# Batch 0's first loads cut to three tokens of queries, g loaded as rows, units of the first block reordered, four product tiles moved behind the next block's start

## The chip, the cores and the metric

The kernel runs on one core of a Trainium2 chip. Its engines are TensorE (PE in the profile; PEld is its weight load), VectorE (DVE), ScalarE (ACT), GpSimd (POOL) and SyncE (SP); the loads and stores run on DMA queues that SP, ACT and POOL fill. The metric is the device time of one execution in microseconds (us); lower is better.

## What is computed

Attention with a squared ReLU in place of the softmax, then a feed-forward layer on the normalised tokens, with a residual:

```python
# q, k, v: (8, 12, 448, 64) float32
scores = scale * np.matmul(q, k.transpose(0, 1, 3, 2))        # scale = 1 / sqrt(64)
attn = np.maximum(scores, 0.0) ** 2 / S                        # S = 448
x = np.matmul(attn, v)                                         # -> x (8, 448, 768)
...
mu = np.mean(x, axis=-1, keepdims=True)
var = np.mean((x - mu) ** 2, axis=-1, keepdims=True)
xn = (x - mu) / np.sqrt(var + 1e-06) * g_ln
ch = np.maximum(xn @ w_ch1, 0.0) @ w_ch2                       # 768 -> 3072 -> 768
return x + ch
```

## The kernel before

**Groups and tokens.** The eight batches have twelve heads each. The heads are taken in groups of four: group n is batch n // 3, part m = n % 3, and each batch has G = 3 groups. On the chip a group's q, k or v is a tile of 128 partitions by 2 x 448 columns: two pairs of heads (r = 0, 1), and in each J = 7 "tokens" of D = 64 columns. So a slice of tokens, such as tokens 0 to 2, is 192 columns of each of the two halves; in the source it is a run of 768 bytes per row of a pair, where the whole is 1,792.

**Loads.** Group 0 of batch 0 is fetched in float32 into a staging tile, q by SP's queue and k by ACT's (L149-150), and cast to bf16 afterwards by DVE, ACT and POOL (`cast`, L156-158; POOL casts tokens 3 to 6 of q, L166). All other loads cast on their way and are issued by POOL in the order of L160-171: q and k of groups 1 and 2, v of groups 0 to 2, twelve parts of the weight w1 (six column chunks of 512, two halves each), then group 3 and the next ones. POOL waits now and then before it issues a load: the eleventh went out when the third had landed. `qbuf[m]` holds the queries of part m of batch 0; it has 64 zeroed columns at either end. The vector g is loaded by SP in two transfers, each of 4-byte pieces, straight into `g_sb` (L173-177), and scaled on DVE by `scale_g`.

**Transposes.** Scores need q and k transposed. For batches 0 and 1 PE does that (`transposes`, `piece`): two transposes for each token into PSUM, and a copy by DVE or ACT back to SBUF. For group 0, `idle` matmuls on ones fill PE before the data comes (30, then 2, then 3).

**Blocks.** Batch 0 and batch 1 are cut along the query tokens into two blocks each: batch 0 into query tokens 0 to 2 (`FIRST`) and 3 to 6. A block is a list of units (`attention_block`): for each of its three groups a unit with the scores of key tokens 0 to 3 and a unit with those of 4 to 6, between them (first block of a batch only) the transposes of the next group, then the product with v of the previous group (`values`), and at the end `last` (the last product) and `centre`, which sums over the features by matmuls with ones (L387) and corrects `xc`, the input of the feed-forward layer, in six DVE operations (L393). `scores` leaves the ReLU to ACT (L320) and the squares to DVE: they are put on a list (`later`) and issued by `squares_now`, at the start of a unit, or after one or two product tiles. In `FIRST` nothing else is there for PE, and `busy` puts matmuls between the scores (L285); their input is `qbuf[0][:, D:D + S]`, that is, one half of group 0's queries with all seven tokens. In `FIRST`, tokens 3 to 6 of group 0's queries are transposed just before the last product (L444); those of groups 1 and 2 with all the others of their group.

**Products.** `ffn1_head` makes product tiles 0 to 2 of the first weight together, `ffn1` one tile after the other (six matmuls, L525), so a block has 22 units for 24 tiles. Tiles 20 to 23 need the last chunk of w1. `ffn1` gives the ReLU to DVE (L531) or ACT (L533): `since` counts the tiles since the last scores, and the first one or two go to DVE.

**Order of the work.** All engines run their instructions in the order in which the program puts them. `interleave(main, side, free, ahead)` puts `ahead` side units in front, spreads the others over the main units, and leaves the last `free` main units without any. The program is: the units of `FIRST` one after the other (L626-629); the 22 product units of `FIRST` with the block of query tokens 3 to 6 at their side (L630); w2's loads, into the space that batch 0's working tiles held; the product units of that second block with batch 1's first block at their side (L637), and so on. The second weight's product (`ffn2`, L563) starts at 101.6 us.

PSUM tiles come from two pools: `ps_mm` with two buffers (product tiles, `busy`, transposes of batch 0, the sum of `FIRST`) and `ps_sc` with three (scores, products with v, transposes of batch 1, `idle_ps`).

```python
def busy(n):
    ps = ps_mm.tile([P, 512], fp32, tag="mm", name="busy_ps")
    for _ in range(n):
        nc.tensor.matmul(ps[:, :S], ones, qbuf[0][:, D:D + S], start=True, stop=True)
```

Of the kernel before, what the change touches and what calls it, by code (L numbers as in the profile page):

```python
# [12 lines left out]
def interleave(main, side, free=0, ahead=0):  # L13


    for unit in side[:ahead]:
        unit()
    side = side[ahead:]
    n, done = len(main) - free, 0
    for i, unit in enumerate(main):  # L20
        unit()
        want = min(len(side), (len(side) * (i + 1)) // n)
        while done < want:
            side[done]()
            done += 1
# [3 lines left out]
def kernel(  # L29
# [22 lines left out]
    nc = tc.nc  # L52
    P = 128
    HP = 64
    bf16 = mybir.dt.bfloat16
    fp32 = mybir.dt.float32

    B, H, S, D = q.shape
# [3 lines left out]
    J = S // HP  # L62
    NP = H // 2
    G = NP // 2
    NB = 2 * J + 1
    K1 = d_model // P
# [9 lines left out]
    const = ctx.enter_context(tc.tile_pool(name="const", bufs=1))  # L76
# [16 lines left out]
    nc.vector.memset(ones, 1.0)  # L93


    srcs = {
        n: [t[b].rearrange("(r hh) (p j) d -> (hh p) r (j d)", hh=2, p=HP) for b in range(B)]
        for n, t in (("q", q), ("k", k), ("v", v))
    }
    qkv = {}  # L100
# [7 lines left out]
    def load(n, names):  # L108
        if n >= len(groups):
            return  # L110
        b, m = groups[n]
        for name in names:
            if b == 1 and name != "v":
                o = (2 * m + "qk".index(name)) * 2 * S
                t = hold[:, o:o + 2 * S].rearrange("p (r s) -> p r s", r=2)
            elif name == "q":
                t = qbuf[m][:, D:D + 2 * S].rearrange("p (r s) -> p r s", r=2)
            else:
                t = io.tile([P, 2, S], bf16, tag=name, name=name + "_sb", bufs=4 if name == "v" else 3)
            nc.gpsimd.dma_start(t, srcs[name][b][:, m:NP:G, :])  # L120
            qkv[name, b, m] = t
# [13 lines left out]
    def load_w1(i):  # L135
        s = slice(i * NCH, (i + 1) * NCH)
        for hf in range(2):
            nc.gpsimd.dma_start(w1[hf * HP:(hf + 1) * HP, :, s], w1_src[hf][:, :, s])
# [4 lines left out]

    stage = hpool.tile([P, K2, S2], bf16, tag="hT", name="stage_sb")
    stage = stage.rearrange("p a n -> p (a n)")[:, :8 * S].bitcast(fp32)
    stage = stage.rearrange("p (i r s) -> p i r s", i=2, r=2)
    for i, (queue, name) in enumerate(((nc.sync, "q"), (nc.scalar, "k"))):  # L149
        queue.dma_start(stage[:, i], srcs[name][0][:, 0:NP:G, :])  # L150

    nc.scalar.activation(spool.tile([P, 1], fp32, tag="root", name="root"), eps_sb, ACTF.Sqrt)
    qkv["q", 0, 0] = qbuf[0][:, D:D + 2 * S].rearrange("p (r s) -> p r s", r=2)
# [2 lines left out]
    def cast(copy, name, lo, hi):  # L156
        s = slice(lo * D, hi * D)
        copy(qkv[name, 0, 0][:, :, s], stage[:, "qk".index(name), :, s])

    load(1, "qk")  # L160
    make_identity(nc, identity)
    load(2, "qk")
    load(0, "v")
    load(1, "v")
    load(2, "v")
    cast(nc.gpsimd.tensor_copy, "q", 3, J)  # L166
    for i in range(6):
        load_w1(i)
    load(3, "qkv")
    load(4, "qk")  # L170
    load(5, "qk")

    g_sb = const.tile([P, K1], fp32)  # L173
    g_src = moe_g_ln.rearrange("(hf c p) -> hf p c", hf=2, p=HP)
    with nc.allow_non_contiguous_dma(reason="one vector of 768"):
        for hf in range(2):
            nc.sync.dma_start(g_sb[hf * HP:(hf + 1) * HP, :], g_src[hf])
    g_mean = const.tile([P, K1], fp32)
    g_score = const.tile([P, K1], fp32)

    def scale_g():
        nc.vector.tensor_scalar_mul(g_mean, g_sb, -1.0 / d_model)
        nc.vector.tensor_scalar_mul(g_score, g_sb, score_scale)

# [3 lines left out]
    def idle(n):  # L188

        for _ in range(n):  # L190
            nc.tensor.matmul(idle_ps[:, 0, :P], ones, ones, start=True, stop=True)
# [1 line left out]
    xT, xc = {}, {}  # L193
    st = {}

    def piece(sb, b, m, n, cuts):
        if b == 0:
            ps = ps_mm.tile([P, 1024], bf16, tag="mm", name="tr_ps")
        else:
            ps = ps_sc.tile([P, 2, 1024], bf16, tag="sc", name="tr_ps")[:, 0]  # L200
        src, i = qkv[n, b, m], "qk".index(n)
        for copy, lo, hi in cuts:
            for j in range(lo, hi):
                for pr in range(2):
                    nc.tensor.transpose(  # L205
                        ps[pr * HP:(pr + 1) * HP, j * P:(j + 1) * P],
                        src[:, pr, j * D:(j + 1) * D], identity)
        for copy, lo, hi in cuts:
            copy(sb[:, i * J + lo:i * J + hi, :],
                 ps[:, lo * P:hi * P].rearrange("p (j c) -> p j c", c=P))  # L210

    def transposes(b, m):


        if b == 0:
            o = 12 * 1024 + m * 2 * J * P
            sb = early[:, o:o + 2 * J * P].rearrange("p (i c) -> p i c", c=P)
        elif m:
            o = (m - 1) * 2 * J * P
            sb = hold[:, o:o + 2 * J * P].rearrange("p (i c) -> p i c", c=P)  # L220
        else:
            sb = tpool.tile([P, NB, P], bf16, tag="qT", name="qT_sb")
        dve, act = nc.vector.tensor_copy, nc.scalar.copy
        if (b, m) == (0, 0):

            cast(dve, "q", 0, 3)
            cast(act, "k", 0, 3)
            cast(act, "k", 3, J)
            idle(30)
            piece(sb, b, m, "q", ((dve, 0, 3),))  # L230
            idle(2)
            piece(sb, b, m, "k", ((dve, 0, 3), (dve, 3, J)))
            idle(3)
        elif b == 0:
            piece(sb, b, m, "q", ((dve, 0, J),))
            piece(sb, b, m, "k", ((dve, 0, 3), (act, 3, J)))
        else:
            piece(sb, b, m, "q", ((dve, 0, J),))
            piece(sb, b, m, "k", ((dve, 0, J),))
        squares_now()  # L240
        st[b, m] = {
            "q": lambda i, r: sb[:, 0:J],
            "k": lambda i: sb[:, J + i],
            "where": lambda pr, j: (j, pr),
            "attn": [], "sb": sb}
# [27 lines left out]


    FULL = (0, J)
    BLK = (((0, 3), (3, J - 3)), ((0, 4), (4, J - 4)))
    FIRST = (0, BLK[0][0])
    n_early = [0]

# [13 lines left out]
    def squares_now(n=None):  # L293


        if n is None or n in [k for k, _ in later]:
            for _, a in later:
                nc.vector.tensor_mul(a, a, a)
            later.clear()
# [116 lines left out]
    def attention_block(b, blk):  # L416


        lo, hi, first = b * G, b * G + G, blk[0] == 0
        units = [lambda: transposed(lo)] if first else []  # L420

        def unit(n, part):
            squares_now()
            for i in range(4 * part, min(4 * part + 4, J), 2):
                if (b, blk) == FIRST and (n == G - 1 or n and i == 2):
                    busy(1)
                scores(n, tuple(range(i, min(i + 2, J))), blk)
            if (b, blk) == FIRST and part and n == hi - 1:
                squares_now()
            if b == 1 and not first and part and n == hi - 1:  # L430
                transposed(hi)
            if part and n > lo:
                values(n - 1, blk)
                if not first:
                    load(n + 3, "v")
        for n in range(lo, hi):
            units.append(lambda n=n: unit(n, 0))
            if first and n + 1 < hi:
                units.append(lambda n=n: transposed(n + 1))
            units.append(lambda n=n: unit(n, 1))  # L440

        def last():
            if (b, blk) == FIRST:
                piece(st[0, 0]["sb"], 0, 0, "q", ((nc.scalar.copy, 3, J),))  # L444
            values(hi - 1, blk)
            if (b, blk) == FIRST:
                busy(2)
            if b == 1 and not first:
                load(hi + 3, "v")
        units.append(last)  # L450
        units.append(lambda: centre(b, blk))
        return units
# [148 lines left out]
    def ffn1_units(b, blk=FULL):  # L601
        if blk == FULL:
            return [lambda ni=ni: ffn1(b, ni, blk) for ni in range(K2)]
        return [lambda: ffn1_head(b, blk)] + [lambda ni=ni: ffn1(b, ni, blk) for ni in range(3, K2)]
# [18 lines left out]


    pairs = B // 2
    for i, unit in enumerate(attention_block(0, BLK[0][0])):  # L626
        if i == 2:
            scale_g()
        unit()
    interleave(ffn1_units(0, BLK[0][0]), attention_block(0, BLK[0][1]), 3, 1)  # L630
    w2 = wpool.tile([P, K2, d_model], bf16, tag="w2", name="w2")
    for i in range(4):
        load_w2(w2, i, 4)
    load(6, "qkv")
    load(7, "qk")
    load(8, "qk")
    interleave(ffn1_units(0, BLK[0][1]), attention_block(1, BLK[1][0]), 3, 1)  # L637
    interleave(ffn1_units(1, BLK[1][0]), attention_block(1, BLK[1][1]), 3, 1)
    tokens(0)
    transposed(by_dma * G + 1)  # L640
# [45 lines left out]
```

## Time and profile before

| what | value |
|---|---|
| median of 3 runs | 552.45 us (551.58 to 556.33) |
| the profiled execution | 551.32 us, its span 549.5 us |
| PE busy | 538.7 us, 98% of the span |
| PEld, DVE, ACT, POOL busy | 318.3, 266.0, 260.2, 109.2 us |
| mean granted clock of PE | 0.997 |
| DMA | 56.62 MB moved, 51.91 MB of it read from HBM |

Busy time by stretch of the same execution, in us (PE, DVE, ACT), with the granted clock and what the DMA engines moved:

| stretch | PE | DVE | ACT | clock | GB/s |
|---|---|---|---|---|---|
| 0 to 5 us | 3.38 | 0.47 | 1.49 | 1.00 | 186 |
| 5 to 10 | 3.70 | 2.13 | 2.54 | 0.81 | 179 |
| 10 to 15 | 4.34 | 4.34 | 4.27 | 0.85 | 204 |
| 15 to 20 | 4.29 | 4.25 | 3.95 | 1.00 | 207 |
| 20 to 25 | 4.59 | 2.71 | 3.64 | 1.00 | 205 |
| 25 to 30 | 4.63 | 4.16 | 4.19 | 1.00 | 206 |
| 30 to 35 | 5.00 | 4.44 | 4.78 | 1.00 | 207 |
| 35 to 40 | 4.76 | 3.34 | 2.58 | 1.00 | 204 |
| 50 to 60 | 10.00 | 6.58 | 8.28 | 1.00 | 211 |

How to read it: block `FIRST` runs from the first scores at 7.86 us to the sum at 20.41; its product units and the second block of batch 0 fill the time to 41.5 us. The DMA figures count what is written: a load that casts reads float32 and writes half as many bytes, so 205 GB/s of such loads are 410 GB/s read. In the timeline each line gives the start and the length of a run of equal instructions, the engine, the line, the operation, its output and inputs and, in brackets, how long the engine was idle before and what ended that.

### The profile page before, as it was taken

The page shows a single profiled execution, that of the slowest core. Times are in us where ns is not written, and L with a number is a line of the kernel's source. Part 1 is how long each engine was busy: PE and PEld are TensorE (multiplying, and loading weights), DVE is VectorE, ACT ScalarE, POOL GpSimd, SP SyncE. Part 2 cuts the span into 40 slices and gives each one's busy share as a digit, 9 for nine tenths or more (in the row PEclk, how much of TensorE's full clock was granted, in tenths as well). Part 3 has the DMA queues.
Part 4 walks back from the last instruction along what each step waited for, and adds up shares of the span by engine and source line. Part 5 has one row for each costly group of instructions (what it writes and reads, how often), then busy time and mean ns, then how long its engine had stood idle before and what let it go on. Part 6 is the DMA issues. An engine that isn't in the chain of part 4 may idle for free.

```text
span 549.5 us, 10988 instructions
## 1 busy us (share of the span) xinstructions
PE 538.7 (98%) x4734; PEld 318.3 (58%) x4734; DVE 266.0 (48%) x511; ACT 260.2 (47%) x424; POOL 109.2 (20%) x135
## 2 busy tenths in 40 slices
PE   7899999999999999999999999999999999999997
PEld 5687779655555555555555555555555555555655
DVE  4776753378886250057777532027687670001111
ACT  5776775455553444455545344445545244440000
POOL 7334102024426100003614400001230400000000
PEclk8999999999999999999999999999999999999999
DMA  9999999979999900028999960006941250001222
GB/s 188 207 204 208 210 194 148 117 116 162 164 176 127 212 2 1 0 59 144 123 142 160 173 124 1 0 1 91 170 102 30 60 100 0 1 0 30 58 57 58
DMA packets 107216, 56.62 MB, mean 103 GB/s; under 512 B 77216, under 2 KB 103712, under 8 KB 107168
## 3 DMA queue, kind: packets, MB, share of 16 engines
q1 hardware_dynamic: 79680, 29.77, 32.3%
q0 software_dynamic: 26976, 25.50, 31.7%
q8 instruction: 37, 0.61, 0.5%
q10 hardware_dynamic: 512, 0.66, 0.3%
q14 instruction: 11, 0.09, 0.1%
HBM read 51.91 MB, written 11.01 MB: 115 GB/s over the span
## 4 chain that ended last, share of the span: by engine, by line
PE 90%; DMA 8%; issue 0%; POOL 0%; DVE 0%; SPq 0%; POOLq 0%
PE o_ps L563 38%; PE h_ps L525 38%; PE sc_ps L309 6%; DMA w<-in_moe_w_ch_dram 5%; PE av_ps L339 5%; DMA qT_sb<-q_sb 2%; PE o_ps L588 1%; DMA q_sb<-in_q_dram 1%; PE h_ps L547 1%; PE sum_ps L387 1%; PE tr_ps L205 0%; POOL k_sb L120 0%; POOL q_sb L120 0%; DVE o_sb L591 0%; POOL identity masks.py:199 0%
## 5 line engine op out<-in xcount | busy, mean ns | idle before, releaser
L525 PE MATMUL h_ps<-xc_sb,w 128*128 128x448 bf16 (+2 forms) x1368 | 219.2, 318 | 0.6 <-DVE hT_sb L531 0.4
L563 PE MATMUL o_ps<-w,hT_sb 128*128 128x384 bf16 x1296 | 219.6, 326 | 0.0
L525 PEld LDWEIGHTS <-w 128*128 128x128 bf16 x1368 | 128.6, 98 | 86.9 <-issue 3.1
L563 PEld LDWEIGHTS <-hT_sb 128*128 128x128 bf16 x1296 | 123.1, 98 | 94.2 <-issue 16.0
L320 ACT ACTIVATE attn_sb<-sc_ps 128x896 bf16<-128x896 f32 (+4 forms) x150 | 126.4, 902 | 84.6 <-PE sc_ps L309 84.6
L533 ACT ACTIVATE hT_sb<-h_ps 128x448 bf16<-128x448 f32 (+2 forms) x212 | 102.5, 483 | 121.5 <-PE h_ps L525 121.1
L322 DVE TENSOR_TENSOR attn_sb<-attn_sb 128x896 bf16<-128x896 bf16 x126 | 81.5, 654 | 39.1 <-ACT attn_sb L320 38.2
L569 DVE SCALAR_TENSOR_TENSOR o_sb<-o_ps,rstd_sb,xtok_sb 128x384 f32<-128x384 f32 x54 | 33.0, 611 | 49.1 <-PE o_ps L563 48.7
L510 DVE RECIPROCAL rstd_sb<-rstd_sb 128x1 f32<-128x1 f32 (+1 forms) x10 | 1.7, 168 | 98.0 <-ACT rstd_sb L509 98.0
L504 DVE BATCH_NORM_STATS2 stats<-xtok_sb 128x6 f32<-128x384 bf16 x56 | 27.5, 533 | 32.7 <-DMA xtok_sb<-xT_sb 32.7
L370 POOL TENSOR_TENSOR part_sb<-part_sb,xT_sb 128x448 f32<-128x448 f32 x24 | 29.5, 1229 | 66.9 <-DVE xT_sb L346 59.3
L367 POOL TENSOR_TENSOR part_sb<-xT_sb 128x448 f32<-128x448 bf16 x6 | 6.6, 1106 | 168.6 <-DVE xT_sb L346 138.7
L393 DVE SCALAR_TENSOR_TENSOR xc_sb<-total_sb,g_mean,xc_sb 128x448 bf16<-128x448 f32 (+2 forms) x54 | 29.0, 605 | 21.2 <-ACT total_sb L391 21.2
L309 PE MATMUL sc_ps<-qT_sb,kT_sb 64*64 64x448 bf16 x504 | 34.7, 357 | 1.5 <-DMA qT_sb<-q_sb 1.5
L339 PE MATMUL av_ps<-attn_sb,v_sb 64*64 64x448 bf16 (+2 forms) x672 | 32.3, 327 | 0.0
L346 DVE TENSOR_SCALAR xT_sb<-av_ps 128x896 bf16<-128x896 f32 (+2 forms) x30 | 26.9, 900 | 9.4 <-PE av_ps L339 9.4
L352 DVE TENSOR_SCALAR xc_sb<-xT_sb,g_sb 128x448 bf16<-128x448 bf16 (+2 forms) x56 | 28.6, 558 | 1.0
L339 PEld LDWEIGHTS <-v_sb 64*64 64x64 bf16 x840 | 22.9, 107 | 10.6 <-issue 1.6
L120 POOL DMA_DIRECT2D k_sb<-in_k_dram x20 | 14.2, 713 | 47.0 <-DMA kT_sb<-k_sb 37.0
L309 PEld LDWEIGHTS <-kT_sb 64*64 64x64 bf16 x504 | 11.5, 105 | 18.5 <-issue 15.0
L120 POOL DMA_DIRECT2D v_sb<-in_v_dram x24 | 17.4, 729 | 21.7 <-PE av_ps L339 17.9
L320 ACT ACTIVATE early<-sc_ps 128x768 bf16<-128x768 f32 (+3 forms) x24 | 18.3, 827 | 2.7 <-PE sc_ps L309 2.5
(63 smaller groups left out, 196.1 us busy)
## 6 DMA issues: line engine op xcount, KB each, us to landing
out_dram<-o_sb SPq DMA_DIRECT2D x54, 192.0 KB, 3.6
v_sb<-in_v_dram POOLq DMA_DIRECT2D x24, 224.0 KB, 4.9
w<-in_moe_w_ch_dram POOLq DMA_DIRECT2D x12, 384.0 KB, 14.5
w<-in_moe_w_ch_dram POOLq DMA_DIRECT2D x4, 1152.0 KB, 20.0
q_sb<-in_q_dram POOLq DMA_DIRECT2D x20, 224.0 KB, 7.7
k_sb<-in_k_dram POOLq DMA_DIRECT2D x20, 224.0 KB, 7.2
hold_sb<-in_q_dram POOLq DMA_DIRECT2D x3, 224.0 KB, 11.9
hold_sb<-in_k_dram POOLq DMA_DIRECT2D x3, 224.0 KB, 11.1
```

Source lines behind the costliest of these rows:

```text
L120: nc.gpsimd.dma_start(t, srcs[name][b][:, m:NP:G, :])
L309: nc.tensor.matmul(ps[cols, r, o * w:(o + 1) * w], g["k"](i)[rows, cols], g["q"](i, r)[rows, blk[0]:sum(blk), cols], start=True, stop=True)
L320: nc.scalar.activation(a, ps[:, :, :len(slots) * w], ACTF.Relu)
L322: nc.vector.tensor_mul(a, a, a)
L339: nc.tensor.matmul(ps[cols, hh, :w], v_sb[rows, pr, j * D:(j + 1) * D], g["attn"][i][rows, r, :], start=(j == 0), stop=(j == J - 1))
L352: nc.vector.tensor_scalar_mul(xc[b][:, c, of(blk)], xT[b // 2][:, c, of(blk, b)], g_sb[:, c:c + 1])
L370: nc.gpsimd.tensor_add(part[b], part[b], x[:, c])
L393: nc.vector.scalar_tensor_tensor(xc[b][:, c, of(blk)], total, g_mean[:, c:c + 1], xc[b][:, c, of(blk)], op0=ALU.mult, op1=ALU.add)
L525: nc.tensor.matmul(ps[:, :w], w1[:, c, ni * P:(ni + 1) * P], xc[b][:, c, of(blk)], start=(c == 0), stop=(c == K1 - 1))
L533: nc.scalar.activation(hT[pair][:, ni, o:o + w], ps[:, :w], ACTF.Relu)
L563: nc.tensor.matmul(ps[:, :DH], hT[pair][:, ki, t * P:(t + 1) * P], w2[:, ki, cols], start=(ki == 0), stop=(ki == K2 - 1))
L569: nc.vector.scalar_tensor_tensor(o_sb[t][:, cols].rearrange("p (c d) -> p c d", d=D), ps[:, :DH].rearrange("p (c d) -> p c d", d=D), rstd[ ...
```

## The change

The staging of group 0 is cut: q's tokens 0 to 2 by SP's queue, k's tokens 0 to 2 by ACT's, k's tokens 3 to 6 by SP's after q's. Of q, tokens 3 to 6 are no longer staged, but loaded with a cast by POOL, after v of group 2; of groups 1 and 2 POOL loads q's tokens 0 to 2 where it loaded the whole q, and tokens 3 to 6 after the first chunk of w1. POOL's own cast goes. g is loaded as six rows in one transfer and turned on PE by two small float32 matmuls with a 6 x 6 identity, copied and scaled on DVE before the first scores. k's tokens 3 to 6 of group 0 are transposed after the first scores, q's tokens 3 to 6 of groups 1 and 2 in the second block, each directly before the scores of its group (in a buffer of `ps_sc`), those of group 0 before `last`. In `FIRST` the second scores unit of group 0 goes ahead of the transposes of group 1, and the product of group 1 goes ahead of the last scores unit. Of `FIRST`'s product units the last four are taken out of the interleaving (which now runs over 18 units, leaves one free, and still puts one side unit ahead) and follow the first five units of the next block, whose remaining 17 are interleaved with batch 1's first block.

```diff
@@ -93,6 +93,9 @@
     nc.vector.memset(ones, 1.0)
+    BLK = (((0, 3), (3, J - 3)), ((0, 4), (4, J - 4)))
     srcs = {
         n: [t[b].rearrange("(r hh) (p j) d -> (hh p) r (j d)", hh=2, p=HP) for b in range(B)]
         for n, t in (("q", q), ("k", k), ("v", v))
@@ -143,11 +146,18 @@
     stage = hpool.tile([P, K2, S2], bf16, tag="hT", name="stage_sb")
     stage = stage.rearrange("p a n -> p (a n)")[:, :8 * S].bitcast(fp32)
     stage = stage.rearrange("p (i r s) -> p i r s", i=2, r=2)
-    for i, (queue, name) in enumerate(((nc.sync, "q"), (nc.scalar, "k"))):
-        queue.dma_start(stage[:, i], srcs[name][0][:, 0:NP:G, :])
+    FEW = BLK[0][0][1]
+    def load_uncast(queue, name, lo, hi):
+        s = slice(lo * D, hi * D)
+        queue.dma_start(stage[:, "qk".index(name), :, s], srcs[name][0][:, 0:NP:G, s])
+    load_uncast(nc.sync, "q", 0, FEW)
+    load_uncast(nc.scalar, "k", 0, FEW)
+    load_uncast(nc.sync, "k", FEW, J)
     nc.scalar.activation(spool.tile([P, 1], fp32, tag="root", name="root"), eps_sb, ACTF.Sqrt)
     qkv["q", 0, 0] = qbuf[0][:, D:D + 2 * S].rearrange("p (r s) -> p r s", r=2)
@@ -157,28 +167,38 @@
         s = slice(lo * D, hi * D)
         copy(qkv[name, 0, 0][:, :, s], stage[:, "qk".index(name), :, s])
-    load(1, "qk")
+    def load_queries(m, lo, hi):
+        s = slice(lo * D, hi * D)
+        t = qkv["q", 0, m] = qbuf[m][:, D:D + 2 * S].rearrange("p (r s) -> p r s", r=2)
+        nc.gpsimd.dma_start(t[:, :, s], srcs["q"][0][:, m:NP:G, s])
+    load_queries(1, 0, FEW)
+    load(1, "k")
     make_identity(nc, identity)
-    load(2, "qk")
+    load_queries(2, 0, FEW)
+    load(2, "k")
     load(0, "v")
     load(1, "v")
     load(2, "v")
-    cast(nc.gpsimd.tensor_copy, "q", 3, J)
-    for i in range(6):
+    load_queries(0, FEW, J)
+    load_w1(0)
+    load_queries(1, FEW, J)
+    load_queries(2, FEW, J)
+    for i in range(1, 6):
         load_w1(i)
     load(3, "qkv")
     load(4, "qk")
     load(5, "qk")
+    g_rows = const.tile([K1, 2, HP], fp32)
+    nc.sync.dma_start(g_rows, moe_g_ln.rearrange("(hf c p) -> c hf p", hf=2, p=HP))
     g_sb = const.tile([P, K1], fp32)
-    g_src = moe_g_ln.rearrange("(hf c p) -> hf p c", hf=2, p=HP)
-    with nc.allow_non_contiguous_dma(reason="one vector of 768"):
-        for hf in range(2):
-            nc.sync.dma_start(g_sb[hf * HP:(hf + 1) * HP, :], g_src[hf])
     g_mean = const.tile([P, K1], fp32)
     g_score = const.tile([P, K1], fp32)
+    identity_g = const.tile([K1, K1], fp32)
     def scale_g():
+        nc.vector.tensor_copy(g_sb, idle_ps[:, 1, :K1])
         nc.vector.tensor_scalar_mul(g_mean, g_sb, -1.0 / d_model)
         nc.vector.tensor_scalar_mul(g_score, g_sb, score_scale)
@@ -193,8 +213,8 @@
     xT, xc = {}, {}
     st = {}
-    def piece(sb, b, m, n, cuts):
-        if b == 0:
+    def piece(sb, b, m, n, cuts, first=True):
+        if b == 0 and first:
             ps = ps_mm.tile([P, 1024], bf16, tag="mm", name="tr_ps")
         else:
             ps = ps_sc.tile([P, 2, 1024], bf16, tag="sc", name="tr_ps")[:, 0]
@@ -226,13 +246,19 @@
             cast(dve, "q", 0, 3)
             cast(act, "k", 0, 3)
             cast(act, "k", 3, J)
-            idle(30)
+            nc.vector.tensor_copy(identity_g, identity[:K1, :K1])
+            idle(24)
             piece(sb, b, m, "q", ((dve, 0, 3),))
-            idle(2)
-            piece(sb, b, m, "k", ((dve, 0, 3), (dve, 3, J)))
             idle(3)
+            piece(sb, b, m, "k", ((dve, 0, 3),))
+            for hf in range(2):
+                nc.tensor.matmul(
+                    idle_ps[hf * HP:(hf + 1) * HP, 1, :K1], g_rows[:, hf], identity_g,
+                    start=True, stop=True)
+            idle(3)
+            scale_g()
         elif b == 0:
-            piece(sb, b, m, "q", ((dve, 0, J),))
+            piece(sb, b, m, "q", ((dve, 0, FEW),))
             piece(sb, b, m, "k", ((dve, 0, 3), (act, 3, J)))
         else:
             piece(sb, b, m, "q", ((dve, 0, J),))
@@ -273,7 +299,6 @@
     FULL = (0, J)
-    BLK = (((0, 3), (3, J - 3)), ((0, 4), (4, J - 4)))
     FIRST = (0, BLK[0][0])
     n_early = [0]
@@ -421,15 +446,21 @@
         def unit(n, part):
             squares_now()
+            if b == 0 and not first and part == 0 and n:
+                piece(st[0, n]["sb"], 0, n, "q", ((nc.vector.tensor_copy, FEW, J),), False)
             for i in range(4 * part, min(4 * part + 4, J), 2):
                 if (b, blk) == FIRST and (n == G - 1 or n and i == 2):
                     busy(1)
                 scores(n, tuple(range(i, min(i + 2, J))), blk)
+                if (b, blk) == FIRST and n == i == 0:
+                    piece(st[0, 0]["sb"], 0, 0, "k", ((nc.vector.tensor_copy, 3, J),))
             if (b, blk) == FIRST and part and n == hi - 1:
                 squares_now()
+                piece(st[0, 0]["sb"], 0, 0, "q", ((nc.scalar.copy, FEW, J),))
             if b == 1 and not first and part and n == hi - 1:
                 transposed(hi)
-            if part and n > lo:
+            if n > lo and part == (0 if (b, blk) == FIRST and n == hi - 1 else 1):
                 values(n - 1, blk)
                 if not first:
                     load(n + 3, "v")
@@ -438,10 +469,10 @@
             if first and n + 1 < hi:
                 units.append(lambda n=n: transposed(n + 1))
             units.append(lambda n=n: unit(n, 1))
+        if b == 0 and first:
+            units[2:4] = units[3], units[2]
         def last():
-            if (b, blk) == FIRST:
-                piece(st[0, 0]["sb"], 0, 0, "q", ((nc.scalar.copy, 3, J),))
             values(hi - 1, blk)
             if (b, blk) == FIRST:
                 busy(2)
@@ -623,18 +654,21 @@
     pairs = B // 2
-    for i, unit in enumerate(attention_block(0, BLK[0][0])):
-        if i == 2:
-            scale_g()
+    for unit in attention_block(0, BLK[0][0]):
         unit()
-    interleave(ffn1_units(0, BLK[0][0]), attention_block(0, BLK[0][1]), 3, 1)
+    units = ffn1_units(0, BLK[0][0])
+    interleave(units[:-4], attention_block(0, BLK[0][1]), 1, 1)
     w2 = wpool.tile([P, K2, d_model], bf16, tag="w2", name="w2")
     for i in range(4):
         load_w2(w2, i, 4)
     load(6, "qkv")
     load(7, "qk")
     load(8, "qk")
-    interleave(ffn1_units(0, BLK[0][1]), attention_block(1, BLK[1][0]), 3, 1)
+    late, units = units[-4:], ffn1_units(0, BLK[0][1])
+    for unit in units[:5] + late:
+        unit()
+    interleave(units[5:], attention_block(1, BLK[1][0]), 3, 1)
     interleave(ffn1_units(1, BLK[1][0]), attention_block(1, BLK[1][1]), 3, 1)
     tokens(0)
     transposed(by_dma * G + 1)
```

## The prediction

> **What bounds the kernel now.** First the page's chain of waits, by engine, then the same chain in order of time.
>
> ```profile
> PE 90%; DMA 8%; issue 0%; POOL 0%; DVE 0%; SPq 0%; POOLq 0%
> ```
> ```profile
> 3.37 6.30 DMA q_sb<-in_q_dram
> ...
> 9.95 12.69 DMA w<-in_moe_w_ch_dram
> ...
> 22.93 15.63 DMA w<-in_moe_w_ch_dram
> ...
> 38.70 0.66 PE h_ps L525 x6
> ```
>
> After 40 us the chain is matrix work on PE, which the change leaves as it is. Up to 38.70 us the chain runs through loads. So this is a question about the first 40 us, and a microsecond won or lost there stays. Next the timeline of those 40 us.
>
> ```profile
> 7.86 0.71 PE L309 MATMUL sc_ps<-early 64*64 64x192 bf16 x16 [0.18 <-DVE early L209]
> ...
> 11.12 0.52 PE L285 MATMUL busy_ps<-q_sb,ones 128*128 128x448 bf16 x1
> ...
> 11.98 0.36 PE L309 MATMUL sc_ps<-early 64*64 64x192 bf16 x8 [0.34 <-ACT early L320]
> ...
> 13.35 0.66 POOL L138 DMA_DIRECT2D w<-in_moe_w_ch_dram  x1 [0.43 <-DMA v_sb<-in_v_dram]
> ...
> 19.15 0.73 ACT L350 ACTIVATE xc_sb<-av_ps,g_score 128x192 bf16<-128x192 f32 x2 [0.98 <-DVE xT_sb L346]
> ...
> 20.41 0.66 PE L387 MATMUL sum_ps<-xT_sb,ones 128*128 128x192 bf16 x6 [0.95 <-ACT early L209]
> ...
> 26.17 0.62 DVE L531 TENSOR_SCALAR hT_sb<-h_ps 128x192 bf16<-128x192 f32 x2
> 26.57 0.66 PE L525 MATMUL h_ps<-xc_sb,w 128*128 128x192 bf16 x6 [0.37 <-DVE hT_sb L531]
> ...
> 26.70 1.02 DVE L298 TENSOR_TENSOR early<-early 128x1024 bf16<-128x1024 bf16 x2
> ```
>
> The reader is to see three things: the filler matmul of L285 reads q_sb and ran at 11.12 without waiting for a load; the sum of L387, with which block one ends, came at 20.41; and DVE still works on squares at 27.7 that were due from 26.17 on, so it runs about a microsecond behind PE. Last, the clock, by windows of 1 us (PE busy, granted clock, DMA share, GB/s).
>
> ```profile
> 7.00:8.00 1.00, 0.82 (x19) 1.00 1.43 171
> 8.00:9.00 1.00, 1.00 (x26) 0.53 1.29 194
> ...
> 11.00:12.00 1.00, 0.66 (x13) 0.76 1.26 202
> 12.00:13.00 1.00, 1.00 (x34) 1.00 1.28 213
> ```
>
> PE had been idle for 1.59 us before 6.07; from 8 to about 11.3 it was granted half the clock.
>
> **Part one, the shorter first loads.** The first casts (5.65 us) waited for two loads of 459 KB read each. Now two of 197 KB come first. From 2.8 us the transfers ran at about 400 GB/s, so 524 KB less is 1.3 us. If a row of 768 B costs what one of 1,792 B does, nothing is won: the rows are as many (512). I take 1.2. Four of seven key tiles leave the path (8 transposes, 0.3 us, and a DVE copy of 0.35): 0.6. The page "DMA: Bandwidth & Descriptors" of the Trainium skill (Specifications) speaks against the cut: transfers under 512 B miss line rate, and the cut rows arrive as 384 B of bf16. By that rule the two cut query loads would each cost a whole one, some 1 us together by this trace's 1.1 us a load; no row here shows it.
>
> The rows of g replace 768 pieces of 4 bytes; DVE's 1.15 us wait for them at 9.28 cost little, since the transposes it copied next ended only then. Now PE waits for g instead, ahead of the first scores. It comes third on SP's queue, behind 459 KB; with both cut loads that is 655 KB, landed by about 5.2 us at that rate, where PE is near 5.3: 0, at most 1 us. First scores at 7.86 - 1.8 = 6.0.
>
> **Part two, the filler now waits for a load.** `busy` reads columns D to D+S of qbuf[0], all seven tokens. Tokens 3 to 6 used to be cast by POOL from the staged copy (6.93, 0.66 us). Now they are the eighth POOL load, after v 2. That the kernel's waits follow regions, not tiles, the trace shows: h_ps used w1 at 21.57 while w1's last part came at 38.56. From first scores to first filler took 3.3 us, so PE stands there at 9.3.
>
> When does the tail land? POOL's eleventh load went out when the third had landed (9.67), so the fourteenth, at 13.35, marks the sixth, v 1: about 13.1. To there 917 + 6 x 459 = 3,670 KB were read; to the tail it is 655 + 2 x 197 + 2 x 459 + 3 x 459 + 262 = 3,606 KB. By pieces: 2,048 rows and 768 of g, now 2,816 rows, the same. So 13.1; 12.3 if g's pieces cost the 0.7 us by which the rate sags below 205 GB/s between 5 and 8 us, 14.3 if short rows cost full ones. PE stands still for 3.8 us; behind the filler are queued scores of group 1, all of group 2 and both products.
>
> From 13.1: filler to scores 0.3, scores and six query transposes to 14.0. DVE then has, without a gap, two copies (0.36 each), two squares (0.51 each), xT 0.55, two xc 0.63, squares 0.51 and 0.31: 17.7. Only then can the product of group 1 run, which the change puts ahead of the last scores: 0.8, xT 0.55, then ACT's two xc (0.73; L350 waited for xT before, too), and behind these in ACT's queue the last two activations, 0.65 and 0.36: 20.8. Square 0.3, product 0.8, xT 0.55: 22.5, against 20.41. **+2.1** (0.5 if only ACT's queue counted, which resumes at 13.6 instead of 13.06; 2.8 with the late tail). The 0.95 us before L387, ACT's copy, is gone and is in this.
>
> The clock: 1.59 us idle brought 3.3 us at half; 3.8 us idle should do it again. The same work took 0.96 against 0.58 (14 transposes). From the filler to the end of the first product is some 2.7 us at full clock, 4.3 at half; part is hidden behind DVE. **+1.0** (0 to 2). The page "TensorE: Matmul & The Clock Gate" (Part 1) says that the gate drops after an idle window of about 3.4 us and opens after a busy one; the drop after 1.59 us was earlier than that rule says. By it alone the cost could be 0.
>
> **Part three, the postponed query tiles.** Two times 8 transposes come into block two: 0.3 us each, **+0.6**. They stand directly ahead of the scores that need them, with only DVE's copy between. DVE has that copy behind its evictions and squares: at the first place PE arrives at 26.57, transposes to 26.9, DVE free at 27.7, copy 0.4, scores at 28.2. That is 1.3 us with nothing else for PE. The second, behind xT 0.69, xc 0.48 and squares 1.02, about 0.9. **+2.2** (0.6 to 3).
>
> **Part four, the last four tiles.** They free PE of w1's last part: the wait at 38.70 goes, **-0.25**; with block one late, no other load binds (the parts landed 0.8 to 1.4 us ahead of use). But between the sum of block two and the head that needs its corrections stood three units and 28 transposes, 2.6 us; now it is one unit, 0.66. The first correction ends 0.85 after the sum and six take 2.47, paced at 0.41 against 0.35 on PE: **+0.5** (0.2 to 1.2). The next block's ten side units fall on 14 main units in place of 19; ACT was 8.3 of 10 us busy there: **+0.2** (0 to 1). The late tiles' own work is only moved. w2 is needed at 101; POOL's load at 65.34 waited for one of its four parts, 5 to 6 us apart, so it is there by about 71 and its delay is covered by 30 us.
>
> Sum: 2.1 + 1.0 + 0.6 + 2.2 - 0.25 + 0.5 + 0.2 = 6.35 us. The profiled execution took 551.3; 551.3 + 6.35 = **557.7**. The median shown is 1.1 above that execution, its lowest 0.3; I leave the number.
>
> **Rivals.** *The hold is cheap* (full clock, and DVE has caught up while PE stood, so each copy costs 0.3 us): 2.1 + 0.6 + 0.6 - 0.25 + 0.5 + 0.2 = 3.75, so 555.1. For it: every engine drains during the hold. Against: DVE is refilled by the first squares.
> *Not slower: PE isn't held at L285.* It would take a tail that has landed by 9.3 us, or no wait for it. Then block one ends about 3.8 us earlier than above (22.5 - 3.8 = 18.7), a gain of 1.7. Block two is then paced by w1's parts, whose arrival hardly moves and which had 0.8 to 1.4 us of slack; the copies fall into those waits, and about 0.9 is left, less 0.5 at the head: 551.3 - 0.4 = 550.9. Against it: 3.6 MB by 9.3 us is over 500 GB/s, which no window shows.
> *The hold is dear*: tail at 14.3, half clock for two stretches, copies at their upper ends: +9.5, so 560.8.
>
> **How the numbers follow.** The forecast 0.50 (its own range 555.5 to 560), cheap 0.22, not held 0.15, dear 0.13. Range 551.8 to 560.3, leaving out about half of the not-held and half of the dear case. About 1% (5.5 us) is what a measurement of this kernel can tell from no change; the bound is 558.0. Slower by more: just over half of the forecast (0.28) and the dear case, 0.41. Faster by more would need 5.5 us in a stretch that holds 1.7: 0.02. Within: 0.57.
>
> **What would show it.** Right: a PE idle of some 4 us before the first L285, ended by a q_sb load; half clock after it; L387 near 23; in block two PE waiting at L309 for DVE's L209. Wrong: a first L285 without a wait, L387 before 20, or no new waits of PE between 25 and 45 us.

## The result, and the profile after

| | before | after |
|---|---|---|
| median of 6 runs | 553.09 us (550.99 to 556.33) | 560.76 us (560.31 to 563.26) |
| the profiled execution, its span | 551.32, 549.5 us | 560.31, 558.5 us |
| sum of block one | 20.41 us | 25.82 us |
| first matmul of the second weight's product | 101.47 us | 112.16 us |

The ratio is 1.0152, with a 95% interval of 1.0123 to 1.0181: slower by over 1%. The page's chain of waits by engine, after:

```profile
PE 94%; DVE 2%; DMA 2%; POOL 1%; issue 0%; ACT 0%; POOLq 0%
```

DMA's share of the chain fell from 8% to 2%, and the kernel is slower all the same. The same chain in order of time (start, us, engine, what) shows what stands in its place:

```profile
6.92 9.14 DMA q_sb<-in_q_dram
16.11 0.55 PE busy_ps L310
...
25.98 0.50 PE sum_ps L412 x6
...
32.14 0.93 DVE early L323 x2
33.46 0.63 PE sc_ps L334 x16
...
47.90 0.49 DVE xc_sb L418
48.44 2.47 PE h_ps L578 x18
```

One load of queries, issued at 6.92 us, carries the chain for 9.14 us, to the filler (now L310). Twice more the chain goes over DVE to PE, at 32 and at 48 us. The timeline, in brackets how long the engine was idle before and what ended that:

```profile
16.11 0.55 PE L310 MATMUL busy_ps<-q_sb,ones 128*128 128x448 bf16 x1 [5.07 <-DMA q_sb<-in_q_dram]
17.37 0.96 PE L225 MATMUL tr_ps<-identity,k_sb 128*64 128x128 bf16 x14
...
25.82 0.66 PE L412 MATMUL sum_ps<-xT_sb,ones 128*128 128x192 bf16 x6
...
33.46 0.63 PE L334 MATMUL sc_ps<-early 64*64 64x256 bf16 x16 [1.56 <-DVE early L229]
...
39.60 0.63 PE L334 MATMUL sc_ps<-early 64*64 64x256 bf16 x16 [1.15 <-DVE early L229]
...
48.44 2.47 PE L578 MATMUL h_ps<-xc_sb,w 128*128 128x256 bf16 x18 [0.48 <-DVE xc_sb L418]
...
74.24 0.64 PE L364 MATMUL av_ps<-attn_sb,v_sb 64*64 64x256 bf16 x12 [0.59 <-DVE attn_sb L323]
```

PE is held 5.07 us by the load; waits 1.56 and 1.15 us for DVE's copies of the postponed query tiles (L229); and 0.48 us for the correction at the head of the next block. None of these waits was there before. Two distances divide the loss: **A**, the sum of block one, came 5.41 us later; **B**, from that sum to the second weight's product, grew from 81.06 to 86.34 us, by 5.28. Within B all of it lies ahead of the sum of batch 1's first block (44.37 us after the sum of block one before, 49.65 now); from there to the second product it is 36.69 us in both.

Of these 10.7 us the time shows 9.0 (by the two profiled executions) or 7.7 (by the medians). What is missing in the profiled executions, 1.7 us, is met near 280 us for the most part, where PE waited 1.5 us for transposed queries before and not at all after.

### The profile page after: what moved, and what is told of

It reads as the page before. It is cut to its first block, busy times and chain, and to the rows that moved or that the text cites. A ratio compares the mean times of both kernels' runs of the same rounds, so it can differ in the third digit from the quotient of the medians.

```text
span 558.5 us, 10989 instructions
## 1 busy us (share of the span) xinstructions
PE 542.1 (97%) x4733; PEld 319.6 (57%) x4733; DVE 266.7 (48%) x515; ACT 261.0 (47%) x424; POOL 111.4 (20%) x137
## 3 DMA queue, kind: packets, MB, share of 16 engines
HBM read 51.91 MB, written 11.01 MB: 113 GB/s over the span
## 4 chain that ended last, share of the span: by engine, by line
PE 94%; DVE 2%; DMA 2%; POOL 1%; issue 0%; ACT 0%; POOLq 0%
PE o_ps L594 39%; PE h_ps L556 38%; PE sc_ps L334 7%; PE av_ps L364 6%; DMA q_sb<-in_q_dram 2%; PE h_ps L578 1%; PE o_ps L619 1%; PE sum_ps L412 1%; DVE early L323 1%; PE tr_ps L225 1%; DVE xT_sb L371 0%; POOL v_sb L123 0%; PE busy_ps L310 0%; DVE xc_sb L377 0%; POOL k_sb L123 0%
## 5 line engine op out<-in xcount | busy, mean ns | idle before, releaser
L594 PEld LDWEIGHTS <-hT_sb 128*128 128x128 bf16 x1296 | 123.1, 98 | 94.3 <-issue 16.1
L334 PEld LDWEIGHTS <-kT_sb 64*64 64x64 bf16 x504 | 11.5, 105 | 16.8 <-issue 13.3
```

The costliest lines, as they stand in the source:

```text
L334: nc.tensor.matmul(ps[cols, r, o * w:(o + 1) * w], g["k"](i)[rows, cols], g["q"](i, r)[rows, blk[0]:sum(blk), cols], start=True, stop=True)
L594: nc.tensor.matmul(ps[:, :DH], hT[pair][:, ki, t * P:(t + 1) * P], w2[:, ki, cols], start=(ki == 0), stop=(ki == K2 - 1))
```

## The experiments

All start from the kernel after, but for two that start from the one before. For each: the filler's first matmul, the sum of block one, the start of the second product, B, PE's wait near 280 us, all from one profiled execution (us); then the median and the ratio to the kernel before, run beside it on the same chip (its medians beside e1 to e12 were 551.4 to 552.1 us, so rows are compared by the ratio).

| kernel | filler | sum | 2nd product | B | wait at 280 | median | ratio, 95% |
|---|---|---|---|---|---|---|---|
| before | 11.12 | 20.41 | 101.47 | 81.06 | 1.5 | 553.09 | |
| after | 16.11 | 25.82 | 112.16 | 86.34 | 0 | 560.76 | 1.0152 (1.0123 to 1.0181) |
| e1 filler reads keys | 11.19 | 21.07 | 107.41 | 86.34 | 2.5 | 558.46 | 1.0106 (1.0060 to 1.0152) |
| e2 whole queries | 15.09 | 25.41 | 111.75 | 86.34 | 0.7 | 561.36 | 1.0165 (1.0130 to 1.0201) |
| e3 tiles a unit earlier | 15.38 | 25.01 | 109.45 | 84.44 | 1.8 | 561.89 | 1.0178 (1.0143 to 1.0213) |
| e4 late tiles back | 15.22 | 24.72 | 107.84 | 83.12 | 1.2 | 557.89 | 1.0108 (1.0069 to 1.0147) |
| e5 hold filled | 15.69 | 23.95 | 110.31 | 86.36 | 0 | 561.75 | 1.0162 (1.0121 to 1.0202) |
| e6 before + tail | 15.44 | 25.68 | 106.28 | 80.60 | 1.9 | 556.18 | 1.0068 (1.0046 to 1.0090) |
| e9 = e1+e3+e4 | 11.01 | 20.73 | 102.77 | 82.04 | 1.6 | 553.49 | 1.0031 (1.0004 to 1.0058) |
| e10 = e9 + order | 11.20 | 19.60 | 102.25 | 82.65 | 2.4 | 552.93 | 0.9999 (0.9972 to 1.0027) |
| e11 first loads only | 11.17 | 18.78 | 101.43 | 82.65 | 2.3 | 551.98 | 1.0006 (0.9988 to 1.0023) |
| e12 before + late tiles | 11.01 | 20.47 | 103.56 | 83.09 | 0.7 | 553.75 | 1.0048 (1.0028 to 1.0069) |

**e1: the filler reads keys, which have landed.** Only what fills PE there is changed.

```diff
-        nc.tensor.matmul(ps[:, :S], ones, qbuf[0][:, D:D + S], start=True, stop=True)
+        nc.tensor.matmul(ps[:, :S], ones, qkv["k", 0, 0][:, 0, :], start=True, stop=True)
```

> The changed kernel, but the filler matmuls of L285 (L310 in the changed kernel) read group 0's keys, which are cast by 5.7 us, in place of its queries. Theory (the hold at the filler is the largest loss): PE's 5.1 us wait at the filler is gone, PE's clock isn't halved after it, and the sum that ends block one (25.82 us in the changed kernel, 20.41 before) comes at about 20; time about 555, that is 5.5 us under the changed kernel and 2 over the one before. Rival (DVE and ACT set the pace of block one anyway, and PE only waits for them elsewhere): the sum comes at about 24 and the time is 558 to 559.

Its timeline:

```profile
11.19 0.56 PE L310 MATMUL busy_ps<-k_sb,ones 128*128 128x448 bf16 x1
...
21.07 0.66 PE L412 MATMUL sum_ps<-xT_sb,ones 128*128 128x192 bf16 x6
...
282.87 0.96 PE L334 MATMUL sc_ps<-qT_sb,kT_sb 64*64 64x448 bf16 x8 [2.48 <-DMA qT_sb<-q_sb]
```

The hold is gone, and A with it, all but 0.66 us (the sum was expected at about 20, by the rival at 24); B is unchanged to the hundredth. The filler starts at 11.19 without a wait, though the tail landed at 13.5 us in this profile. So the load held PE through the filler's operand alone. The time, 558.46, lies in the rival's range all the same, for another reason: of the 4.75 us won at the front the profiled execution kept 0.5. PE waited 2.48 us at 282 us, where after it didn't wait, and then ran at half the clock (window: length, PE busy, granted clock, DMA share, GB/s):

```profile
282.00:283.00 1.00, 0.13 (x4) 0.89 1.32 246
283.00:284.00 1.00, 1.00 (x9) 0.50 1.30 229
...
286.00:287.00 1.00, 1.00 (x7) 0.90 1.28 258
```

That is 3.4 us at half, or 1.7 us lost by an engine that is busy. The same is seen in e3, e10 and e11. From the start of the second product to the end, the wait at 280 taken off, it is 447.9 to 448.2 us in these four, where the clock fell after waits of 1.81 to 2.48 us, and 446.3 to 446.8 us in the other eight profiles, where it stayed at 1.00 (e6 waited 1.90 us and kept it). The four runs of e1 spread from 555.74 to 559.81.

**e2: the queries of groups 1 and 2 loaded whole**, which puts 524 KB more of source ahead of the tail, in as many rows.

```diff
-    load_queries(1, 0, FEW)
-    load(1, "k")
+    load(1, "qk")
...
-    load_queries(2, 0, FEW)
-    load(2, "k")
+    load(2, "qk")
...
-    load_queries(1, FEW, J)
-    load_queries(2, FEW, J)
```

> The changed kernel, but the queries of groups 1 and 2 are loaded whole where it loads three tokens of them, and their later loads are dropped. Theory (a short row costs a DMA engine nearly what a full one costs): the tail of group 0's queries lands when it did, 16.1 us, within 0.5, and the time is 560 to 561. Rival (bytes set the pace): 524 KB more are read ahead of the tail, 1.3 us at 410 GB/s, so it lands at 17.4 and the time is about 562.

```profile
15.09 0.55 PE L306 MATMUL busy_ps<-q_sb,ones 128*128 128x448 bf16 x1 [4.92 <-DMA q_sb<-in_q_dram]
```

The tail landed just ahead of that, at 15.0 us: sooner than the theory's 16.1 and far from the rival's 17.4. But one profile of each can't decide here. Seven kernels load exactly as the change does up to the tail, and in their profiles it landed at 13.5 (e1), 14.2 (e10), 15.2 (e4, e9), 15.3 (e3), 15.6 (e5) and 16.1 us (after); e11 loads as e2 does, 15.0. So no gain of the cut rows is seen, against a spread of 2.5 us that has another cause. What a short row costs is read better from the packets (last section).

**e3: the postponed tiles one unit earlier**, so that DVE's copy has a unit to hide behind.

```diff
-            if b == 0 and not first and part == 0 and n:
-                piece(st[0, n]["sb"], 0, n, "q", ((nc.vector.tensor_copy, FEW, J),), False)
+            if b == 0 and not first and part and n + 1 < hi:
+                piece(st[0, n + 1]["sb"], 0, n + 1, "q", ((nc.vector.tensor_copy, FEW, J),), False)
```

> The changed kernel, but the postponed query tiles of groups 1 and 2 are transposed one scores unit earlier in block two, so that DVE's copy has a unit's time. Theory (DVE's copy behind its squares holds PE): the two waits of PE at the scores, 1.56 and 1.15 us, go, and the time is 2 to 2.7 us lower, about 558. Rival (block two is bound by DVE and ACT): the waits reappear at the products or at the PSUM buffers, and the time is within 0.7 us of 560.8.

```profile
31.19 0.63 PE L334 MATMUL sc_ps<-early 64*64 64x256 bf16 x16
...
34.91 0.96 PE L364 MATMUL av_ps<-early,v_sb 64*64 64x256 bf16 x28 [0.53 <-DVE early L229]
```

The scores no longer wait; 0.53 us is left ahead of a product. B fell by 1.9 us. The total didn't, it is above the 558 expected and above the kernel after: the wait at 284 us was 1.81 in this profile, with 1.9 more lost behind it (half clock, as in e1). What the tiles cost is shown at the front, not in the time.

**e4: the last four tiles back in the block's own order.**

```diff
-    interleave(units[:-4], attention_block(0, BLK[0][1]), 1, 1)
+    interleave(units, attention_block(0, BLK[0][1]), 3, 1)
...
-    late, units = units[-4:], ffn1_units(0, BLK[0][1])
-    for unit in units[:5] + late:
-        unit()
-    interleave(units[5:], attention_block(1, BLK[1][0]), 3, 1)
+    interleave(ffn1_units(0, BLK[0][1]), attention_block(1, BLK[1][0]), 3, 1)
```

> The changed kernel, but the last four product tiles of the first block stay where they were before the change, and both interleavings are as before. Theory (with block one late, w1 has landed and the move only costs): the 0.5 us wait of the head, its slower pace (0.4) and the waits in the denser block of batch 1 (0.8) go; time about 559. Rival (the move pays by taking w1's last part off the path): the time is 561 or more.

```profile
30.83 0.66 PE L556 MATMUL h_ps<-xc_sb,w 128*128 128x192 bf16 x6 [0.37 <-DVE hT_sb L562]
...
32.37 0.63 PE L334 MATMUL sc_ps<-early 64*64 64x256 bf16 x16 [0.53 <-DVE early L229]
```

B fell by 3.2 us, the largest part of it, and the time follows: the rival falls. The second product starts 4.3 us sooner, the other 1.1 of it ahead of the sum of block one, where the tail landed 0.9 us sooner in this profile. One more product tile stands ahead of the first postponed query tiles, so PE waits 0.53 us for their copy, and not 1.56. **e12** is the counterpart: these lines of the change alone, put into the kernel before.

> The kernel before with one part of the change alone: the last four product tiles of the first block go behind the first five units of the next. Theory (what it frees PE of is 0.2 us, and it makes the neighbouring stretches denser and uncovers the head's wait): the second weight's product starts 2.5 to 3.3 us later, at 104 to 104.8, and the time rises by 2 to 3.5 us. Rival (it only cost in the changed kernel, where DVE was behind): within 1 us of before.

Its timeline at the next block's head:

```profile
39.83 2.46 PE L547 MATMUL h_ps<-xc_sb,w 128*128 128x256 bf16 x18 [0.48 <-DVE xc_sb L393]
```

B grew by 2.0 us and the time by 0.48% (2.7 us). The head waits 0.48 us and takes 2.46 in place of 2.14; three further waits of PE, for squares and a copy of DVE (0.26, 0.17 and 0.59 us), make 1.8 together, against 0.4 that went (the wait for w1, and part of one for an eviction). The remaining 0.6 us isn't resolved. So the move costs 2.0 us by itself and 3.2 beside the rest of the change; of the 1.2 between them 1.0 is the longer wait for the first postponed tiles (1.56 against 0.53 in e4).

**e5: PE kept busy through the hold** with 80 small matmuls on ones.

```diff
+    def fill(n):
+        ps = ps_mm.tile([P, 512], fp32, tag="mm", name="fill_ps")
+        for _ in range(n):
+            nc.tensor.matmul(ps[:, :P], ones, ones, start=True, stop=True)
...
+                    if n == 1:
+                        fill(80)
```

> The changed kernel with 80 more matmuls of 128 x 128 on ones ahead of the first filler, so that PE works through most of its wait for the tail. Theory (the halved clock after the hold costs time by itself): the transposes and scores after the filler run at full clock (20 transposes in 0.8 us in place of 1.3), the sum of block one comes 1 to 1.5 us after where it came, relative to the filler's start (25.82 - 16.11 = 9.7 in the changed kernel, so 8.2 to 8.7), and the second weight's product starts at about 111. Rival (DVE and ACT hide the slow clock): still 9.4 to 9.7 us from filler to sum.

```profile
15.69 0.36 PE L310 MATMUL busy_ps<-q_sb,ones 128*128 128x448 bf16 x1 [1.28 <-DMA q_sb<-in_q_dram]
16.47 0.56 PE L225 MATMUL tr_ps<-identity,k_sb 128*64 128x128 bf16 x14
...
23.95 0.66 PE L417 MATMUL sum_ps<-xT_sb,ones 128*128 128x192 bf16 x6
```

Filler and transposes took 0.36 and 0.56 us in place of 0.55 and 0.96, and from filler to sum it is 8.26 us in place of 9.71. So the half clock after the hold costs 1.45 us by these two profiles. The profiled execution was 1.7 us shorter (558.62); the median of five runs was not.

**e6: the tail alone, in the kernel before**: of the staged queries only tokens 0 to 2, and tokens 3 to 6 loaded by POOL in the place of its cast.

```diff
-    for i, (queue, name) in enumerate(((nc.sync, "q"), (nc.scalar, "k"))):
-        queue.dma_start(stage[:, i], srcs[name][0][:, 0:NP:G, :])
+    nc.sync.dma_start(stage[:, 0, :, :3 * D], srcs["q"][0][:, 0:NP:G, :3 * D])
+    nc.scalar.dma_start(stage[:, 1], srcs["k"][0][:, 0:NP:G, :])
...
-    cast(nc.gpsimd.tensor_copy, "q", 3, J)
+    nc.gpsimd.dma_start(qkv["q", 0, 0][:, :, 3 * D:], srcs["q"][0][:, 0:NP:G, 3 * D:])
```

> The kernel before with one part of the change alone: tokens 3 to 6 of group 0's queries aren't staged and cast by POOL, but loaded with a cast by POOL after v of group 2. Theory (the filler's read of the tail is what holds PE): PE waits at the filler of L285 from about 11 to about 15.5 us, and the sum of block one comes at 24 to 25 in place of 20.4; the second weight's product starts at 105 to 106 in place of 101.5. Rival (the hold comes from the cut loads of groups 1 and 2 or from the new order of the units): PE waits less than 1 us there and the sum stays at 20 to 21.

```profile
15.44 0.55 PE L285 MATMUL busy_ps<-q_sb,ones 128*128 128x448 bf16 x1 [5.83 <-DMA q_sb<-in_q_dram]
```

Three lines bring back nearly the whole of A: a hold of 5.83 us and a sum at 25.68, against 25.82. The start of the second product is 4.8 us later, the time 0.68% (3.8 us).

**e9, e10: the three undone together, then the order of group 1's product too.** e9 holds the edits of e1, e3 and e4; e10 has, besides,

```diff
-            if n > lo and part == (0 if (b, blk) == FIRST and n == hi - 1 else 1):
+            if n > lo and part:
```

> The changed kernel with three parts undone: the fillers read keys, the postponed query tiles are transposed one unit earlier, the last four product tiles stay in place. Theory (these three make up the loss, and add): the second weight's product starts at 112.2 - 4.8 - 1.9 - 3.3 = 102.2 us, against 101.5 in the kernel before, and the time is within 1 us of before, give or take PE's wait for a transposed load near 280 us. Rival (a fourth loss is left, or they overlap): the product starts at 104 or later.

> The kernel with the three parts undone, and the product of group 1 again after the last scores unit of block one instead of ahead of it. Theory (that order puts ACT's two xc operations, which wait for DVE, ahead of the last two activations): the sum of block one comes 0.5 to 1.5 us sooner than without, and the second weight's product starts at 101 to 101.5. Rival (the order doesn't matter, since DVE's squares end last either way): within 0.3 us of the kernel with the three parts undone.

In e9 the second product starts 9.4 us earlier than after, and e1's share of A with e3's and e4's of B makes 4.75 + 1.9 + 3.2 = 9.85: the parts add up, within half a microsecond, and 1.3 us against the kernel before is left. In e10 the sum comes 1.13 us sooner than in e9, so the product's place cost a microsecond in A; half of it reaches the second product. Its time is that of the kernel before.

**e11: only the shorter first loads, g as rows and the reordered units** (e1, e2, e4 and e10's order, and all seven tokens of queries transposed at once).

> What is left of the change when the parts that lost are undone: the short staged loads of group 0, g as rows, the keys' tail after the first scores and the reordered units of group 0 stay; the fillers read keys, the queries of groups 1 and 2 are loaded and transposed whole, the last four tiles stay in place, the product of group 1 comes after the last scores. Theory (the early start is worth something once nothing waits for the tail): block one's sum comes at 19.8 to 20.4, PE waits less than 0.7 us for DVE in block two, and the second weight's product starts at 100.7 to 101.5; the time is 0 to 0.8 us under the kernel before, too little to be sure of. Rival (the last part of w1 lands at 38.5 whatever PE does): the product starts no sooner than 101.5 and the time is the same within 0.3 us.

```profile
18.78 0.66 PE L408 MATMUL sum_ps<-xT_sb,ones 128*128 128x192 bf16 x6
22.90 0.66 PE L550 MATMUL h_ps<-xc_sb,w 128*128 128x192 bf16 x6 [0.42 <-DMA w<-in_moe_w_ch_dram]
...
38.65 0.66 PE L550 MATMUL h_ps<-xc_sb,w 128*128 128x192 bf16 x6 [0.80 <-DMA w<-in_moe_w_ch_dram]
```

Block one ends 1.6 us earlier than before, and PE then waits 1.5 us for parts of w1 (0.42, another 0.27 and 0.80); the second product starts at 101.43, against 101.47. With nothing else in the way the gain at the start is taken by the loads of w1: the sum came sooner than expected, the product and the time as the rival had it. No version tried beats the kernel before by more than the measurement tells.

## Why the prediction was right or wrong

The direction and the places were right; the size was too small by 3 us, and the time lies just above the range. Two terms of the sum were mis-sized.

**The first loads, right.** The first cast started 1.6 us sooner, for 1.2 predicted (before, then after):

```profile
5.65 0.36 DVE L158 CAST q_sb<-stage_sb 128x384 bf16<-128x384 f32 x1 [4.38 <-DMA stage_sb<-in_q_dram]
4.03 0.36 DVE L168 CAST q_sb<-stage_sb 128x384 bf16<-128x384 f32 x1 [2.75 <-DMA stage_sb<-in_q_dram]
```

**The landing of the tail (13.1 us), wrong.** It came at 16.06. The step that failed is the equation of bytes ahead with time. The DMA view of the kernel after, cut at 12.80 and at 16.06 us (queue, kind: packets, MB written, share of 16 engines):

```profile
q0 software_dynamic: 2125, 1.47, 82.7%
...
q0 software_dynamic: 2823, 2.12, 91.0%
```

Ahead of the tail, and with it, stand 2,951 KB of casting loads, 1.48 MB written. The queue had moved that much by 12.8 us, as predicted, but not those bytes: by 16.06 it had moved 0.64 MB more, which can only be loads issued behind the tail. How much overtakes differs from profile to profile with the same loads. In e1 the tail's own line, from issue to landing 6.6 us, and the queue at that landing (13.5 us) read

```profile
q_sb<-in_q_dram POOLq DMA_DIRECT2D x1, 128.0 KB, 6.6
...
q0 software_dynamic: 2351, 1.65, 85.6%
```

so 0.17 MB overtook, and the tail came within half a microsecond of the 13.1; in e10 it was 0.26 MB, in e3, e4, e5 and e9 0.44 to 0.57. The more overtook, the later the landing. With whole rows, 1.74 MB ahead, e2 at 15.04 us reads

```profile
q0 software_dynamic: 2479, 2.05, 88.5%
```

and 0.31 MB overtook. The mark that I took, v 1 in the trace of before, had 0.15 MB of later loads in it (1.53 MB moved by 13.1 us, 1.38 ahead), which I didn't count; 0.64 less 0.15 at 0.205 MB a microsecond is 2.4 of the 3.0 us. The trace of before could have warned: its POOL saw v 2 land 1.83 us after v 1, where 459 KB at 410 GB/s are 1.1. Late landings at that place were thus there before the change. What lets later loads overtake wasn't tried. One thing stands in the view up to 16.06 us and not in that up to 12.80: `q8 instruction: 1, 0.02, 0.4%`, about 1 us of one of the 16 engines (0.4% of 16 times 16.06 us, an estimate); that it held back a load's last part isn't shown.

**Block one, +3.1 predicted, +5.41 measured,** by the landing. From the release to the sum 9.4 + 1.0 were predicted and 9.71 measured, but as 8.26 without the half clock (e5) and 1.45 by it: two errors that partly cancel, which is luck. That PE would be held at the filler, and by which load, was right, and e1 and e6 show it from both sides. PE reached the filler at 11.04, not at 9.3: its work ran at half speed over the first 10 us of this execution (six transposes in 0.53 us, 0.36 before), so the idle time was 5.07 us and not longer. Where it ran at full speed from 5 us on, PE was through with the scores ahead of the filler at about 9.8 (e4, e5).

**The windows after the hold** show the clock (window: length, PE busy, granted clock, DMA share, GB/s):

```profile
12.00:13.00 1.00, 0.00 (x0) 1.00 1.43 220
13.00:14.00 1.00, 0.00 (x0) 0.80 1.18 192
14.00:15.00 1.00, 0.00 (x0) 0.50 1.27 204
...
19.00:20.00 1.00, 1.00 (x28) 0.50 1.25 204
20.00:21.00 1.00, 1.00 (x14) 0.78 1.25 206
```

The clock fell to half some 2.6 us into the hold (0.80 in the window from 13 to 14) and came back in the window from 20 to 21 us: 6.8 us at half, the first 2.5 with PE idle. Predicted +1.0 (0 to 2), measured 1.45.

**The postponed tiles, +2.8 predicted:** their two waits were 1.56 and 1.15 (2.7 with them, against 2.2); putting them earlier gave back 1.9. Right, to the reason.

**The last four tiles, +0.45 predicted (-0.25, +0.5, +0.2), wrong in size:** 2.0 alone, 3.2 beside the rest. The head was right in kind (wait of 0.48 us; with the slower head 0.8, against 0.5). What failed is the denser stretch at 0.2: after the head PE waits for DVE twice (0.17 and 0.59 us), ahead of it once (0.26), and 0.6 more is lost that no wait shows. The 3.2 also contain 1.0 us more of waiting for the first postponed tiles: two parts meet there, which the sum has as separate terms. I had reasoned there from ACT's load alone; DVE was the engine that fell behind.

**Rivals.** That the hold is cheap falls (copies and clock cost no less than the forecast said). That PE isn't held falls. The dear case gave the measured number, 560.8, by another sum, so by luck: its tail landed at 14.3, and neither the 2.0 us of the last four tiles nor the stage near 280 us is in it.

**What no step foresaw:** the stage near 280 us, where PE waits 0 to 2.5 us for transposed queries, differently in each profile. It took back 1.5 us of the loss in the kernel after. In e1 and e3 wait and half clock together took 4.3 and 3.7 us, most of the one's gain and more than the other's. At the start of the second product the forecast is 4.3 us short (10.7 measured, 6.35 predicted), at the end 3. What decides the length of that wait stays open.

## What to carry to other kernels

A matmul that only fills time has operands, and its waits are as real as any other's: let it read something that landed long ago. When a load is split, bytes ahead of it over the rate give the earliest landing of its second half, not the likely one, since later loads share the rate (13.1 us by bytes, 13.5 to 16.1 in seven profiles); and look for the next load that binds before counting on an earlier start (here w1's parts took all of 1.6 us). Work moved out of a block's end isn't only moved: it was the cover between a sum and the first use of its correction, and the place that it goes to loses the slack by which another engine kept up.

## What the runs showed of the hardware

- **A short row costs less than a long one, but not by its bytes.** The DMA view of the kernel after from 6 to 7 us, then from 7 to 8:

```profile
DMA packets 302, 0.14 MB, mean 138 GB/s; under 512 B 241, under 2 KB 302, under 8 KB 302
...
q0 software_dynamic: 302, 0.14, 133.6%
...
DMA packets 168, 0.14 MB, mean 139 GB/s; under 512 B 17, under 2 KB 168, under 8 KB 168
...
q0 software_dynamic: 168, 0.14, 105.8%
```

By share over packets that is 71 and 101 ns each (an estimate). In the packets of the trace the median is 51 ns for 384 B (three tokens), 60 for 512, 88 for 896 (a whole row) and 98 for 1,024. The Trainium skill, "DMA: Bandwidth & Descriptors" (Specifications), says that transfers under 512 B miss line rate; 384 B in 51 ns against 896 in 88 agrees, but there is no jump between 384 and 512. That a cut load would cost a whole one, as the prediction took from this rule, isn't in the page's words and isn't so here. The low rate of this stretch isn't their doing alone: it lasts through the microsecond that has almost none.
- **Loads of one queue overtake:** 0.15 to 0.64 MB of later loads were moved before an earlier one had landed, 0.17 to 0.64 with the very same loads issued.
- **Half clock came in stretches of 3.4 us:** from 8.1 to 11.5 us in the kernel before, once in e1 at 283 us, twice that (6.8 us) after the long hold. Idle times of 1.59 (before) and 1.81 to 2.48 us (near 280) brought it, others up to 1.90 us (e6) didn't.
- **The clock is not always in its column.** At 4 to 10 us of the kernel after the granted clock reads 1.00, and six transposes take 0.53 us, 14 take 0.96; at full speed 14 take 0.56 to 0.58. In e2, e4 and e5 the stretch from 5 us on ran at full speed; in e1 14 transposes took 0.96 us even at 12.46, with 1.00 granted: executions differ here. Durations, not the column, tell the speed so early.
